# First tiles of both batch elements first, other-tile bias tables behind, and the softmax scaling on VectorE

## The chip, the cores and the metric

One core of one Trainium2 chip runs the whole program in one launch. The metric is device time in microseconds (us), the median of three runs of the same program. Engines: PE (TensorE matmul), PEld (its weight loads), DVE (VectorE), ACT (ScalarE), POOL (GpSimd) and SP (SyncE, which here only starts transfers).

## The reference

Attention with global and local keys and distance biases, then a dense gated feed-forward, then a feed-forward of one expert per token.

```
scores = q @ k.T / sqrt(64) - slope[h] * dist      # dist = n_local for global keys out of the window
keep   = (key < n_global) | (0 <= row - key < n_local)       # 8 and 96
x      = softmax(scores where keep) @ v                      # 2 batch elements, 8 heads, 768 rows
y      = (silu(x @ w_gate) * (x @ w_val)) @ w_out            # 1536 tokens, 512 -> 1536 -> 512
e      = argmax(y @ r_gate)
out    = p[e] * sigmoid(y @ r_out)[e] * relu(y @ w1[e]) @ w2[e]
```

## The kernel before, in words

**Tiles.** The rows of each batch element are six tiles of 128: tiles 0 to 5 and 6 to 11. With 96 local and 8 global keys a tile needs its own keys and those of one other tile: the tile before it, whose first 32 columns are overwritten by the first 32 keys of the batch element. The first tile of a batch element (0 and 6) needs its own keys only. Its scores are 128 wide, those of all others 256.

**Steps.** The loop at L781 makes 48 steps of attention, four for each of twelve positions (a pair of heads `j` of position `i`). Before the change position i is tile i. A step s issues, in this order: the scaling by the row sums of step s-1 (`att_R`), the tables `scale_tab`, the scores of step s (`att_S`), the products with v of step s-4 (`att_V`), the transposes of the exponentials of step s-3 (`att_P`), and in two of four steps the transposes of the next position's k and q (`att_T`). `att_X` turns a finished position into the input of the first feed-forward, and `load_qk` and `load_v` fetch later ones.

**Scores.** `att_S` (L283) multiplies in three parts, because k and q are split into a high and a low part (`khi`, `klo`, `qh`, `ql`) for accuracy. Each head of a pair has one bank (`ps_s0`, `ps_s1`) with no second buffer, so the scores of a step wait until VectorE's pass over the step before (L287: adds the bias table, takes the row minimum `mn`) has read the bank. ScalarE takes the exponential (L291) with its row sums `sm`; `att_R` has VectorE make 1/sum (`rs`, L227 and L320) and GpSimd multiply both heads by it:

```
nc.gpsimd.tensor_tensor(out=sp[:, :, 0:nw], in0=sp[:, :, 0:nw], in1=rs.to_broadcast([P, 2, nw]), op=ALU.mult)
```

**Bias tables.** `tab` holds own, other and own distances side by side (L233 to L241), `tab0` those of a first tile. `scale_tab(j, 0)` has ScalarE scale `tab0` for two heads; `scale_tab(j, 1)` has VectorE scale `tab`, 384 wide, in steps `TL` to `TL + 3`, with `TL = 2`.

**Beside it.** Weights come as 1 MB pieces of 64-bit numbers that are made 32-bit in four passes: L352 on ScalarE, L353, L358 and L361 on VectorE; L369 and L370 then split them. Up to step 13 (`GO`) PE gets start-up matmuls (`spin`, L147) between these; from step 13 on each step also issues two or three pieces of the first feed-forward (`m1_up` L387, `m1_down` L418 to L420), whose part `lo` is made on GpSimd (L399) in its first third. From step 13 every second step has SP write zeros to a buffer (`clear_rows`, L461). SP's transfers are issued in order: loads of q, k and v, `clear_rows`, and the reload of the first 32 rows of v (L332) for each position that is not a first tile. GpSimd issues the weight loads (L121) and copies the first 32 keys (L276, L277).

**Order.** The engines' instruction lists come from a scheduler that takes the program's order as a priority and moves instructions forward that are ready early. Within an engine the list is fixed.

The change touches `bt`, `load_v`, `att_T`, `window`, `att_S`, `att_R`, `att_V`, the table code and the loop:

Of the kernel before, what the change touches and what calls it, by code (L numbers as in the profile page):

```python
# [31 lines left out]
def attn_moe_moe_kernel(  # L32
# [224 lines left out]
    sp_t = {}  # L257

    def window(i):
        b, t = bt(i)  # L260
# [4 lines left out]
        own_first = s < o
        lo, hi = min(s, o), max(s, o)
        sl = slice(lo, hi + 1, hi - lo)
        return sl, ([0, 1] if own_first else [1, 0]), (tabs[:, :, 0:2 * P] if own_first else tabs[:, :, P:3 * P])

    def att_S(i, j):  # L270
# [997 lines left out]
```

## Time and profile before

| what | us |
|---|---|
| median of three runs | 684.61 |
| lowest and highest run | 683.14, 685.48 |
| span of the profiled execution, first to last instruction | 682.6 |
| PE busy | 656.2 |
| DVE busy | 406.9 |
| ACT busy | 299.3 |
| POOL busy | 134.4 |

The page gives for the profiled execution its span alone and no time of its own beside it. In the rows "x" is a count. [...] "idle before" is the time that the engine stood still, with what ended it.

### The profile page before, as it was taken

Reading aid. Unit: us, or ns where it says so; the run is one execution under the profiler, and the core shown is the slowest. Engines: PE = TensorE matmul, PEld = TensorE weight load, DVE = VectorE, ACT = ScalarE, POOL = GpSimd, SP = SyncE. Lnnn points to the kernel's source line nnn. Section 1 sums busy time; section 2 is a strip of 40 time slices with the busy share of each in tenths; the row PEclk is TensorE's granted clock in tenths of the full one; section 3 lists DMA queues with packets and bytes.
Section 4 is the critical chain, followed back from the end, with each engine's and each line's share of the span. In section 5 each row is a group of like instructions: output and inputs, shape, how many; then the busy total and the mean of one; then the engine's idle time right before and its main releaser. Section 6 shows DMA issues by size and latency. Waiting matters only on the chain. (4 is left out here: it accounts for less than half of the span.)

```text
span 682.6 us, 12065 instructions
## 1 busy us (share of the span) xinstructions
PE 656.2 (96%) x4645; PEld 571.4 (84%) x4645; DVE 406.9 (60%) x1007; ACT 299.3 (44%) x675; POOL 134.4 (20%) x180
## 2 busy tenths in 40 slices
PE   8999899999999999999999999998989999999993
PEld 7777687777788889999999999996878988998892
DVE  6689797564548887333464545466587656665120
ACT  5487575555535553111342222234466545555110
POOL 3245363433322320000000111011410110011011
PEclk8599999999999999999999999999999999999997
DMA  9666574220005464000040111122798666652000
GB/s 219 155 164 182 178 219 131 65 51 21 21 5 185 127 218 151 1 1 1 16 170 1 63 63 63 48 90 76 245 315 309 214 205 229 223 207 80 0 26 28
DMA packets 70674, 81.30 MB, mean 119 GB/s; under 512 B 43469, under 2 KB 43469, under 8 KB 70608
## 3 DMA queue, kind: packets, MB, share of 16 engines
q1 hardware_dynamic: 62304, 51.06, 24.8%
q0 software_dynamic: 8304, 29.39, 12.5%
q8 instruction: 38, 0.62, 0.4%
q14 instruction: 28, 0.23, 0.1%
HBM read 66.77 MB, written 14.72 MB: 119 GB/s over the span
## 5 line engine op out<-in xcount | busy, mean ns | idle before, releaser
L387 PE MATMUL ps_gv<-xhi,whi 128*128 128x256 f32 x576 | 168.1, 292 | 0.0
L387 PE MATMUL ps_gv<-xlo,whi 128*128 128x256 f32 x576 | 164.4, 285 | 0.0
L387 PE MATMUL ps_gv<-xhi,wlo 128*128 128x256 f32 x576 | 164.1, 285 | 0.0
L387 PEld LDWEIGHTS ps_gv<-xhi,whi 128*128 128x128 f32 x576 | 110.1, 191 | 6.3 <-issue 0.7
L387 PEld LDWEIGHTS ps_gv<-xlo,whi 128*128 128x128 f32 x576 | 110.3, 191 | 3.9 <-issue 1.0
L387 PEld LDWEIGHTS ps_gv<-xhi,wlo 128*128 128x128 f32 x576 | 110.5, 192 | 0.4
L575 DVE TENSOR_TENSOR wlo<-raw,whi 128x512 fp32r<-128x512 f32 (+1 forms) x104 | 81.9, 809 | 33.5 <-ACT whi L572 33.0
L572 ACT CAST whi<-raw 128x512 fp32r<-128x512 f32 (+1 forms) x104 | 72.0, 718 | 54.6 <-PE ps_gv L882 23.7
L394 DVE SCALAR_TENSOR_TENSOR hh<-th,ps_gv 128x256 f32<-128x256 f32 x72 | 30.0, 417 | 83.4 <-ACT th L392 83.4
L392 ACT ACTIVATE th<-ps_gv 128x256 f32<-128x256 f32 x72 | 27.4, 381 | 95.0 <-PE ps_gv L387 94.8
L321 POOL TENSOR_TENSOR sp<-sp,rs 128x512 f32<-128x512 f32 (+1 forms) x48 | 50.4, 1051 | 72.7 <-DVE rs L320 48.6
L882 PE MATMUL ps_gv<-sh,whi 128*128 128x256 f32 x224 | 62.9, 281 | 0.0
L882 PE MATMUL ps_gv<-sh,wlo 128*128 128x256 f32 x224 | 62.8, 281 | 0.0
L882 PE MATMUL ps_gv<-sl,whi 128*128 128x256 f32 x224 | 62.8, 280 | 0.0
L291 ACT ACTIVATE sp<-sp,mn 128x256 f32<-128x256 f32 (+1 forms) x96 | 46.6, 487 | 26.0 <-DVE mn L287 22.3
L398 ACT CAST hi<-hh 128x256 fp32r<-128x256 f32 x72 | 29.1, 405 | 60.7 <-DVE hh L395 56.8
L546 POOL DMA_INDIRECT xs<-ypay,rw x12 | 12.9, 1073 | 211.0 <-DVE rw L230 192.8
L287 DVE CUSTOM_DVE_ANT_0 sp<-ps_s,tabs 128x256 f32<-128x256 f32 (+1 forms) x96 | 35.9, 393 | 16.9 <-PE ps_s L283 16.0
L882 PEld LDWEIGHTS ps_gv<-sh,whi 128*128 128x128 f32 x224 | 42.3, 189 | 0.4
L882 PEld LDWEIGHTS ps_gv<-sl,whi 128*128 128x128 f32 x224 | 42.3, 189 | 0.4
L882 PEld LDWEIGHTS ps_gv<-sh,wlo 128*128 128x128 f32 x224 | 42.4, 189 | 0.0
L418 PE MATMUL ps_y<-whi,hi 128*128 128x512 f32 x96 | 40.1, 417 | 1.1 <-ACT hi L398 1.1
(241 smaller groups left out, 1355.3 us busy)
## 6 DMA issues: line engine op xcount, KB each, us to landing
raw<-in_moe_w_dram SPq DMA_DIRECT2D x30, 1024.0 KB, 5.2
raw<-in_moe_w_out_dram POOLq DMA_DIRECT2D x6, 1024.0 KB, 5.6
raw<-in_moe_w_gate_dram POOLq DMA_DIRECT2D x5, 1024.0 KB, 5.8
raw<-in_moe_w_val_dram POOLq DMA_DIRECT2D x5, 1024.0 KB, 5.8
xs<-ypay SPq DMA_DIRECT2D x8, 514.0 KB, 5.8
xr<-xs POOLq DMA_DIRECT2D x7, 514.0 KB, 5.8
ytok<-ypay SPq DMA_DIRECT2D x12, 257.0 KB, 3.3
ypay<-in_k_dram SPq DMA_DIRECT2D x12, 256.0 KB, 3.7
```

Of the source, the lines that this page charges most:

```text
L287: nc.vector.tensor_tensor_reduce(out=sp[:, e, 0:nw], in0=pS[e][:, 0:nw], in1=tb[:, h0 + e, :], scale=-QS, scalar=3.0e38, op0=ALU.add, op1= ...
L291: nc.scalar.activation(out=sp[:, e, 0:nw], in_=sp[:, e, 0:nw], func=AF.Exp, bias=mn[:, i, h0 + e:h0 + e + 1], scale=-1.0, accum_out=sm[:, ...
L321: nc.gpsimd.tensor_tensor(out=sp[:, :, 0:nw], in0=sp[:, :, 0:nw], in1=rs.to_broadcast([P, 2, nw]), op=ALU.mult)
L387: nc.tensor.matmul(o, a[:, kk, fo:fo + P], x[c][:, kk, :], start=(kk == 0 and m == 0), stop=(kk == KD - 1 and m == 2))
L392: nc.scalar.activation(out=th, in_=pg[:, 0, :], func=AF.Tanh, scale=0.5)
L394: nc.vector.scalar_tensor_tensor(out=hh, in0=th, scalar=1.0, in1=pg[:, 0, :], op0=ALU.add, op1=ALU.mult)
L398: nc.scalar.copy(hi, hh)
L418: nc.tensor.matmul(o, hi[:, sl], wh, start=first, stop=False)
L546: put = [nc.gpsimd.indirect_dma_start(out=xs, out_offset=bass.IndirectOffsetOnAxis(ap=rw[:, z].bitcast(U32), axis=0), in_=pay[:, z], in_of ...
L572: ins = nc.scalar.copy(hv[:, o], raw[:, o])
L575: nc.vector.tensor_tensor(out=lv[:, o], in0=raw[:, o], in1=f(hv[:, o]), op=ALU.subtract)
L882: nc.tensor.matmul(ph[:, fo, :], a[:, kk, fo * P:(fo + 1) * P], x[:, kk, :], start=(kk == 0 and m == 0), stop=(kk == KD - 1 and m == 2))
```

## The change

The positions are tiles 0, 6, 1 to 5 and 7 to 11 in this order. Position 1 is tile 6, a first tile, with 128-wide scores; its keys stay in the buffer `xhi[5]`, its v in `ypay[:, 8]`, until tile 7 (position 7) has used them. Since they don't lie beside tile 7's own keys, `att_S` makes two runs of 128 columns there in place of one of 256. The copies of first keys and the reload of v are left out for the second tile of a batch element, whose other tile holds these already (`t > 1`). `kgh` and `kgl` hold the first keys of both batch elements. `TL` is 4, and the three instructions that make the middle of `tab` are called in step 4. `att_R` multiplies on VectorE, one head at a time. `tokid` and the row numbers of `ytok` follow the new order.

```diff
-TL = 2
+TL = 4
...
+    SEQ = [b * NT for b in range(B)] + [b * NT + t for b in range(B) for t in range(1, NT)]
     def bt(i):
-        return i // NT, i % NT
+        return SEQ[i] // NT, SEQ[i] % NT
+    def prev(i):
+        return SEQ.index(SEQ[i] - 1)
+    def slot(i):
+        return max(0, i - 1) % 3
+    def k_of(i):
+        if i == 1:
+            return xhi[NCH - 1][:, :, 0:P], xhi[NCH - 1][:, :, P:2 * P]
+        return khi[:, slot(i)], klo[:, slot(i)]
...
+    def other_tab():
+        ts(ta, before_, NL, BIG, ALU.is_ge, ALU.mult)
+        tt(tab[:, P:2 * P], ta, before_, ALU.add)
+        ts(tab[:, P:P + GW], tg[:, 0:GW], NL, None, ALU.add)
...
+    def runs_of(i):
+        at = window(i)[0]
+        if len(at) == 1 or 1 in at:
+            return [(n * P, P, *(lambda r, j, k=k: k[r, j, :] for k in k_of(x))) for n, x in enumerate(at)]
+        a, z = (slot(x) for x in at)
+        return [(0, 2 * P, *(lambda r, j, k=k: k[r, a:z + 1:z - a, j, :] for k in (khi, klo)))]
...
-        if j == 0 and t > 0:
-            o = (i - 1) % 3
-            nc.gpsimd.tensor_copy(khi[:, o, :, 0:GW], f(kgh))
-            nc.gpsimd.tensor_copy(klo[:, o, :, 0:GW], f(kgl))
+        if j == 0 and t > 1:
+            o = slot(prev(i))
+            nc.gpsimd.tensor_copy(khi[:, o, :, 0:GW], f(kgh[:, b]))
+            nc.gpsimd.tensor_copy(klo[:, o, :, 0:GW], f(kgl[:, b]))
...
-        for m, (a, x) in enumerate(((qh, khi), (qh, klo), (ql, khi))):
-            for e in range(2):
-                r = slice(64 * e, 64 * e + 64)
-                nc.tensor.matmul(pS[e][:, 0:nw], a[r, j, :], x[r, sl, j, :], start=(m == 0), stop=(m == 2))
+        for o, n, kh, kl in runs_of(i):
+            for m, (a, x) in enumerate(((qh, kh), (qh, kl), (ql, kh))):
+                for e in range(2):
+                    r = slice(64 * e, 64 * e + 64)
+                    nc.tensor.matmul(pS[e][:, o:o + n], a[r, j, :], x(r, j), start=(m == 0), stop=(m == 2))
...
-        nc.gpsimd.tensor_tensor(out=sp[:, :, 0:nw], in0=sp[:, :, 0:nw], in1=rs.to_broadcast([P, 2, nw]), op=ALU.mult)
+        for e in range(2):
+            ts(sp[:, e, 0:nw], sp[:, e, 0:nw], rs[:, e, :], None, ALU.mult)
...
-            if t > 0:
-                nc.sync.dma_start(out=v_t[i - 1][0:GW], in_=v[b, :, 0:GW, :].rearrange("h p d -> p h d"))
+            if t > 1:
+                nc.sync.dma_start(out=v_t[prev(i)][0:GW], in_=v[b, :, 0:GW, :].rearrange("h p d -> p h d"))
...
         if TL <= s < NPAIR + TL:
+            if s == TL:
+                other_tab()
             scale_tab(s - TL, 1)
```

How the order moves, first on VectorE at its table of distances, ahead of the first scores. The last three instructions of the tables before `klo`, in the changed kernel (`ypay` is the scratch that holds `tab`, L247 and L250 are the helpers `ts` and `tt`):

```order
L256 SCALAR_TENSOR_TENSOR ypay<-ypay,ng 128x128
L247 TENSOR_SCALAR ypay<-ypay,ng 128x128
L250 TENSOR_TENSOR ypay<-ypay 128x128
L247 TENSOR_SCALAR ypay<-ypay,ng 128x32
L220 TENSOR_TENSOR klo<-ps_y,khi 128x512
L220 TENSOR_TENSOR ql<-ps_y,qh 128x512
L247 TENSOR_SCALAR tabs<-ypay 128x384 x2
```

The three instructions of `other_tab` stand where they stood before, ahead of `klo`, and the first two table scalings directly behind `ql`.

VectorE from step 1's score pass on (`rs` is 1/sum, `sp` the exponentials, `tabs` the scaled tables, ISA rows with `mn` are the score pass), before:

```order
L287 ISA sp,mn<-ps_s_306,tabs 128x128
L287 ISA mn 128x1
L320 RECIPROCAL rs<-rs 128x2
L287 ISA sp,mn<-ps_s_307,tabs 128x128
L287 ISA mn 128x1
L227 TENSOR_SCALAR tabs<-ypay 128x384 x3
L227 TENSOR_SCALAR rs<-sm 128x2
L227 TENSOR_SCALAR tabs<-ypay 128x384
```

and in the changed kernel:

```order
L316 ISA sp,mn<-ps_s_305,tabs 128x128
L316 ISA mn 128x1
L349 RECIPROCAL rs<-rs 128x2
L316 ISA sp,mn<-ps_s_306,tabs 128x128
L316 ISA mn 128x1
L247 TENSOR_SCALAR sp<-sp,rs 128x128 x2
L247 TENSOR_SCALAR tabs<-ypay 128x384 x2
L247 TENSOR_SCALAR rs<-sm 128x2
L247 TENSOR_SCALAR tabs<-ypay 128x384
```

Two multiplies come in behind each score pass, and one of the eight table scalings goes from here to step 4.

PE at the products with v of position 3, with what each row waits for (`vr` are the tiles of v: 761 and 754 the position's own, 572 and 580 the other one, whose first rows are reloaded; DMAHW is a transfer of SP), before:

```order
L387 MATMUL ps_gv_1099<-xhi0_81,wlo_912 128x256
L387 MATMUL ps_gv_1099<-xhi0_81,whi_911 128x256
L337 MATMUL ps_av_1041<-pT_990,vr_572 64x128 [waits DMAHW6_49]
L337 MATMUL ps_av_1041<-pT_990,vr_572 64x128
L337 MATMUL ps_av_1041<-pT_1052,vr_761 64x128 x2
```

and in the changed kernel:

```order
L417 MATMUL ps_gv_1097<-xhi0_81,wlo_907 128x256
L417 MATMUL ps_gv_1097<-xhi0_81,whi_906 128x256
L367 MATMUL ps_av_1038<-pT_986,vr_580 64x128 [waits DMAHW4_49,DVE_49]
L367 MATMUL ps_av_1038<-pT_986,vr_580 64x128
L367 MATMUL ps_av_1038<-pT_986,vr_754 64x128 [waits DMAHW3_49]
L367 MATMUL ps_av_1038<-pT_986,vr_754 64x128
```

The half with the reloaded rows is now the first of the position; before, the own half had been done some 20 rows ahead of it. On SP the reload stands behind a `clear_rows` in both.

## Rows read from the trace of the kernel before

**Rows 1.** The page: span, and part 1, busy us by engine (share, instructions).
```profile
span 682.6 us, 12065 instructions
...
PE 656.2 (96%) x4645; PEld 571.4 (84%) x4645; DVE 406.9 (60%) x1007; ACT 299.3 (44%) x675; POOL 134.4 (20%) x180
```

**Rows 2.** Stretches: length, PE, PEld, DVE, ACT, POOL busy (instructions), PEclk, DMA share, GB/s.
```profile
13.00:32.00 19.00, 19.00 (x111) 14.06 (x109) 13.01 (x39) 10.19 (x30) 5.08 (x8) 0.50 0.80 222
32.00:33.00 1.00, 1.00 (x5) 0.80 (x5) 0.78 (x5) 0.33 (x2) 0.05 (x1) 0.60 0.00 0
...
28.00:75.00 47.00, 43.16 (x333) 33.22 (x332) 42.13 (x106) 32.00 (x79) 22.95 (x25) 0.94 0.61 164
```

**Rows 3.** PE in order of time, 0 to 62 us: start, length, engine, line.
```profile
13.68 0.47 PE L283 MATMUL ps_s<-khi,qh 64*128 64x128 f32 x2
...
14.51 1.25 PE L147 MATMUL ps_gv<-ones 128*128 128x128 bf16 x10
...
28.44 0.58 PE L283 MATMUL ps_s<-khi,qh 64*128 64x256 f32 x1
...
29.38 0.71 PE L147 MATMUL ps_gv<-ones 128*128 128x128 bf16 x5
```

**Rows 4.** VectorE's groups, shapes apart, 28 to 75 us (last row 0 to 60).
```profile
L287 DVE CUSTOM_DVE_ANT_0 sp<-ps_s,tabs 128x256 f32<-128x256 f32 x25 | 10.1, 408 | 1.4 <-PE ps_s L283 1.4
L358 DVE SCALAR_TENSOR_TENSOR raw<-raw 128x1024 int32<-128x1024 int32 x5 | 9.1, 1814 | 0.0
L361 DVE SCALAR_TENSOR_TENSOR raw<-raw 128x1024 int32<-128x1024 int32 x4 | 6.7, 1666 | 0.0
L353 DVE TENSOR_SCALAR raw<-raw 128x1024 int32<-128x1024 int32 x5 | 5.4, 1082 | 0.0
...
L227 DVE TENSOR_SCALAR rs<-sm 128x2 f32<-128x2 f32 x12 | 3.5, 289 | 1.9 <-ACT sp L291 1.9
...
L287 DVE CUSTOM_DVE_ANT_0 sp<-ps_s,tabs 128x128 f32<-128x128 f32 x8 | 2.1, 282 | 0.3 <-PE ps_s L283 0.3
```

**Rows 5.** The same lines over the whole run: ns minimum/median/maximum.
```profile
L358 DVE SCALAR_TENSOR_TENSOR raw<-raw x18: 1200/1227/2057, 17.2 to 260.5; 128x1024 int32<-128x1024 int32 x18
...
L361 DVE SCALAR_TENSOR_TENSOR raw<-raw x18: 1205/1218/2040, 18.6 to 263.8; 128x1024 int32<-128x1024 int32 x18
...
L353 DVE TENSOR_SCALAR raw<-raw x18: 673/687/1434, 15.7 to 259.7; 128x1024 int32<-128x1024 int32 x18
...
L227 DVE TENSOR_SCALAR rs<-sm x48: 148/161/1006, 12.5 to 191.6; 128x2 f32<-128x2 f32 x48
```

**Rows 6.** GpSimd's groups, 28 to 75 us.
```profile
L321 POOL TENSOR_TENSOR sp<-sp,rs 128x512 f32<-128x512 f32 x13 | 15.3, 1177 | 15.8 <-DVE rs L320 13.6 <-PE ps_tr L194 1.6 <-DMA qr<-in_q_dram 0.6
```

**Rows 7.** PE in order of time: scores 128 wide, then 256 wide.
```profile
101.70 0.33 PE L283 MATMUL ps_s<-khi,qh 64*128 64x128 f32 x2
...
102.18 0.50 PE L419 MATMUL ps_y<-wlo,hi 128*128 128x512 f32 x1
...
125.00 0.38 PE L283 MATMUL ps_s<-khi,qh 64*128 64x256 f32 x2
...
125.55 0.39 PE L387 MATMUL ps_gv<-xhi,whi 128*128 128x256 f32 x1
```

**Rows 8.** VectorE in order of time: two table scalings and what follows.
```profile
11.35 0.62 DVE L227 TENSOR_SCALAR tabs<-ypay 128x384 bf16<-128x384 f32 x2
11.89 0.68 DVE L200 TENSOR_TENSOR klo<-ps_tr,khi 128x512 fp32r<-128x512 f32 x1
```

**Rows 9.** Waits of PE, 60 to 250 us: total, times, longest.
```profile
PE ps_y L420 <- POOL lo L399: 1.5, 4, 0.8
```

**Rows 10.** SP's queue, and PE, in order of time, at the longest wait.
```profile
62.64 1.91 SPq L461 DMA_DIRECT2D xs<-ypay  x1
64.65 0.56 SPq L332 DMA_DIRECT2D vr<-in_v_dram  x1
...
73.32 1.17 PE L337 MATMUL ps_av<-pT,vr 128*64 128x128 f32 x12 [2.87 <-DMA vr<-in_v_dram]
```

More of the change, by code (lines that the diff above doesn't have):

```diff
@@ L91, in attn_moe_moe_kernel @@
     xk = [ypay[:, NTILE - 3 + z, 0:DM].rearrange("p (h d) -> p h d", h=H) for z in range(2)]
+    SEQ = [b * NT for b in range(B)] + [b * NT + t for b in range(B) for t in range(1, NT)]
     def bt(i):
-        return i // NT, i % NT
+        return SEQ[i] // NT, SEQ[i] % NT
+    def prev(i):
+        return SEQ.index(SEQ[i] - 1)
+    assert B == 2
+    def slot(i):
[4 more added lines that the diff above has]
+        return khi[:, slot(i)], klo[:, slot(i)]
     q_t, k_t, v_t = {}, {}, {}
@@ L108, in load_v @@
         b, t = bt(i)
-        a = at_p.tile([P, H, HD], F32, tag="vr", name="vr", bufs=3)
+        if i == 1:
+            a = ypay[:, NTILE - 4, 0:DM].rearrange("p (h d) -> p h d", h=H)
+        else:
+            a = at_p.tile([P, H, HD], F32, tag="vr", name="vr", bufs=3)
         nc.sync.dma_start(out=a, in_=v[b, :, t * P:(t + 1) * P, :].rearrange("h p d -> p h d"))
@@ L178, in attn_moe_moe_kernel @@
     klo = at_p.tile([P, 3, NPAIR, P], F32R, name="klo", bufs=1)
-    kgh = at_p.tile([P, NPAIR, GW], F32R, name="kgh", bufs=1)
-    kgl = at_p.tile([P, NPAIR, GW], F32R, name="kgl", bufs=1)
+    kgh = at_p.tile([P, B, NPAIR, GW], F32R, name="kgh", bufs=1)
+    kgl = at_p.tile([P, B, NPAIR, GW], F32R, name="kgl", bufs=1)
     qT = {}
@@ L184, in att_T @@
         b, t = bt(i)
-        s = i % 3
+        kh, kl = k_of(i)
         qs = q_t.pop(i)
@@ L189, in att_T @@
         kr = k_t.pop(i)
-        for src, hi, lo in ((kr, khi[:, s], klo[:, s]), (qs, qh, ql)):
+        for src, hi, lo in ((kr, kh, kl), (qs, qh, ql)):
             yield
@@ L202, in att_T @@
         if t == 0:
-            nc.gpsimd.tensor_copy(kgh, f(khi[:, s, :, 0:GW]))
-            nc.gpsimd.tensor_copy(kgl, f(klo[:, s, :, 0:GW]))
+            nc.gpsimd.tensor_copy(kgh[:, b], f(kh[:, :, 0:GW]))
+            nc.gpsimd.tensor_copy(kgl[:, b], f(kl[:, :, 0:GW]))
     list(att_T(0))
@@ L237, in attn_moe_moe_kernel @@
     nc.scalar.copy(tab[:, 2 * P:3 * P], tab[:, 0:P])
-    ts(ta, before_, NL, BIG, ALU.is_ge, ALU.mult)
-    tt(tab[:, P:2 * P], ta, before_, ALU.add)
-    ts(tab[:, P:P + GW], tg[:, 0:GW], NL, None, ALU.add)
+    def other_tab():
+        ts(ta, before_, NL, BIG, ALU.is_ge, ALU.mult)
+        tt(tab[:, P:2 * P], ta, before_, ALU.add)
+        ts(tab[:, P:P + GW], tg[:, 0:GW], NL, None, ALU.add)
     def scale_tab(j, t):
@@ L260, in window @@
         b, t = bt(i)
-        s = i % 3
         if t == 0:
-            return slice(s, s + 1), [0], tabs[:, :, 3 * P:4 * P]
-        o = (i - 1) % 3
[L265 to L268, printed above, removed]
+            return [i], [0], tabs[:, :, 3 * P:4 * P]
+        if prev(i) == 1 or slot(i) < slot(prev(i)):
+            return [i, prev(i)], [0, 1], tabs[:, :, 0:2 * P]
+        return [prev(i), i], [1, 0], tabs[:, :, P:3 * P]
+    def runs_of(i):
[4 more added lines that the diff above has]
+        return [(0, 2 * P, *(lambda r, j, k=k: k[r, a:z + 1:z - a, j, :] for k in (khi, klo)))]
     def att_S(i, j):
@@ L330, in att_V @@
             av_t[i] = ps_tile("av", [P, NPAIR, P])
-            if t > 0:
-                nc.sync.dma_start(out=v_t[i - 1][0:GW], in_=v[b, :, 0:GW, :].rearrange("h p d -> p h d"))
+            if t > 1:
+                nc.sync.dma_start(out=v_t[prev(i)][0:GW], in_=v[b, :, 0:GW, :].rearrange("h p d -> p h d"))
         av = av_t[i]
         for w, src in enumerate(order):
-            vt = v_t[i] if src == 0 else v_t[i - 1]
+            vt = v_t[i] if src == 0 else v_t[prev(i)]
             for e in range(2):
@@ L456, in attn_moe_moe_kernel @@
     tokid = cst.tile([P, NTILE], I32, name="tokid")
-    nc.gpsimd.iota(tokid, pattern=[[P, NTILE]], base=0, channel_multiplier=1)
+    nc.gpsimd.iota(tokid[:, 0:B], pattern=[[S, B]], base=0, channel_multiplier=1)
+    for b in range(B):
+        o = B + b * (NT - 1)
+        nc.gpsimd.iota(tokid[:, o:o + NT - 1], pattern=[[P, NT - 1]], base=b * S + P, channel_multiplier=1)
     nc.gpsimd.tensor_copy(ids[:, 0:NTILE - 1], tokid[:, 0:NTILE - 1])
@@ L764, in m1_stream @@
                     for z in range(2):
-                        nc.sync.dma_start(out=ytok[(i + z) * P:(i + z + 1) * P, :], in_=ypay[:, i + z, :])
+                        nc.sync.dma_start(out=ytok[SEQ[i + z] * P:(SEQ[i + z] + 1) * P, :], in_=ypay[:, i + z, :])
                     if c == NCH - 2:
```

1 line of the change is left out of this document (removed).

## Prediction

> **What bounds the kernel now.** I read the page first, then the stretches of the granted clock, then PE's instructions in time, then VectorE's groups. The page gives 682.6 us of span, with PE busy for 656.2 of it [rows 1]: from end to end TensorE is the engine that sets the time, and what the change touches lies in the first 135 us or so. A step below is one `att_S`, a pair of heads of one position; there are 48, and position i has steps 4i to 4i+3.
>
> Two things cost PE time early on. [...] Second VectorE: between 28 and 75 us it is busy for 42.13 of 47 us [rows 2], with the score pass, the splitting of weights and all else in one queue, so PE often starts its next scores there when VectorE frees a bank.
>
> VectorE is itself slowed in that stretch. The weight passes L358, L361 and L353 average 1.81, 1.67 and 1.08 us and the two-element L227 0.289 us [rows 4]; their medians over the whole run, most of it with an idle GpSimd, are 1.23, 1.22, 0.69 and 0.161 [rows 5]. The company is GpSimd: its 13 multiplies L321 take 1.18 us each in the stretch [rows 6].
>
> **What the new order does not give.** It only permutes PE's work. By step 33 both programs have issued the same scores (but for one case below), transposes, start-up matmuls and feed-forward matmuls. So a first feed-forward that starts earlier is no gain in itself: four narrow steps early (4 to 7) are repaid by four wide ones at steps 24 to 27. The time changes only by (1) PE work that is added, (2) PE time at the low clock, (3) PE time with nothing to do. Each part of the change is priced as one of these.
>
> **The change part by part.**
>
> *Scores of tile 7 (PE work added).* Its other tile is tile 6, whose keys now lie apart, so a step issues 12 matmuls of 128 columns instead of 6 of 256. Six of 128 take 0.48 us (101.70 to 102.18), six of 256 take 0.55 (125.00 to 125.55) [rows 7]. Twice 0.48 less 0.55 is 0.41; the second six follow matmuls of their own kind, for which I take off 0.1. 0.3 by four steps is **+1.2 us** (ends: 0.3, if only the columns count and they are the same, and 1.6).
>
> *Low clock.* [...]
>
> *Scaling on VectorE.* Two `tensor_scalar` a step, one for each head (128x256, or 128x128 in a narrow step), replace one L321. No row has a VectorE multiply of 256 elements by a column. The nearest is the table scaling, 384 elements: two of them from 11.35 to 11.89, when the next instruction starts [rows 8], so 0.27 us each; I take 0.2 for 256, 0.4 a step. The other end is 0.41 each, the score pass of 128x256, which reads two inputs [rows 4]. For the 13 multiplies of the stretch that adds 5.2 us. Taken away is the company of L321: 5 x 0.59 + 4 x 0.45 + 5 x 0.39 + 12 x 0.13 = 8.3 us of slowing [rows 4, 5]. Of GpSimd's 22.95 busy us there L321 has 15.3 [rows 2, 6]; the rest, part of it only DMA issues, stays, so I count 80%, 6.6 us. Net -1.4. The narrow steps shorten the score pass too: 8 x (0.41 - 0.28) = 1.0 us [rows 4], all of it before 75 us. VectorE has 2.4 us less to do where it is full, and PE gets perhaps 60% of that: **-1.5 us** (ends: -2.4, and +3.1 with 0.41 each, which adds 10.7 for the 6.6 and the 1.0).
> [...]
>
> *GpSimd relieved.* PE waited 1.5 us in four places for `lo` (L399) [rows 9], which queues behind those multiplies of 1.18 us. Without them: **-1.3 us** (ends -1.5 and 0). The weight loads issued from GpSimd and its key copies lose the same neighbours, but they wait for `wlo` of VectorE and for PE, so 0.
>
> *Bias tables later.* By the order of instructions this hardly happens: `other_tab` still stands ahead of the first `klo`, and seven of the eight wide scalings stay ahead of the score pass of step 2; one moves to step 4. 0.
>
> *Loads and copies.* The loads of q, k and v are as many and as large, in the same places of SP's queue. The reload of the first v rows and the two first-key copies go for tiles 1 and 7; PE's waits do not name the copies, and the one long wait on a reload is another's. 0.
>
> *That wait.* PE stood 2.87 us, until 73.32, for 64 KB of v, issued at 64.65 behind a 514 KB `clear_rows` (62.64) on SP's queue [rows 10]. In the new order the reload of position 3 stands behind the same `clear_rows`, and the matmul that needs it comes first among its position's, no longer after the own half. So it stays: 0 (ends -2.9 and +1.5).
>
> Sum: 1.2 - 1.0 - 1.5 - 1.3 = -2.6 us. The profiled execution has a span of 682.6; the median of the three runs is 684.6, 2.0 above, which I leave as it is: **682.0 us**.
>
> **Rivals.**
> *Nothing but a permutation.* The low clock ends at the same moment, and PE, which keeps its order, finds other waits in place of VectorE's. Only +1.2 and -1.3 are left: 684.5. For it: PE is shown busy for 43.16 of the 47 us anyway [rows 2]. Chance 0.23.
> *Both stalls shrink.* [...] Chance 0.17.
> *VectorE becomes the bound (slower).* A multiply costs 0.41, and two stand between two score passes, the second of which frees a bank for PE. Then +3.1 replaces -1.5 and the clock gives nothing: 684.6 + 1.2 - 1.3 + 3.1 = 687.6. It decides from about 0.35 us a multiply. For it: VectorE is 90% busy there already [rows 2]. Against it: the table scaling [rows 8]. Chance 0.11.
> *The clock stays low for longer (slower).* Narrow steps leave PE less between two answers of VectorE, and these come later by the multiplies. PE held 0.50 for 19 us though its rows show no break [rows 2], so a few more microseconds are possible. Each costs half: 7 us more are +3.5, and the -1.0 goes: 686.5. [...] Chance 0.07.
>
> **How the numbers follow.** My forecast has 0.42; its own range is 680.5 to 683.5. No change means within 0.3%, 2.05 us, about what a measurement of this kernel can tell. Of the forecast 0.30 lies below 682.55 and 0.12 above. Faster: 0.30 + 0.17 = 0.47. Same: 0.12 + 0.23 = 0.35. Slower: 0.11 + 0.07 = 0.18. The range goes from 677.0, below both stalls shrunk, to 686.5, and leaves out most of the slower rivals.
>
> **What would show it.** Right: L358, L361 and L353 near their medians between 28 and 75 us, multiplies at 0.2 to 0.3 us, no waits for `lo`, the clock risen by about 30 us, the first feed-forward some 4 us earlier, but step 33 only 2 to 3 us earlier. Wrong: a multiply over 0.35 us from start to start, a granted clock of 0.50 well beyond 33 us, or a wait for v of another size.

## The result and the profile after

The changed kernel is **slower**. Four executions have a median of 691.68 us (690.91 to 694.87), beside 683.88 (682.15 to 685.48) for four of the kernel before: a ratio of 1.0146, 95% interval 1.0104 to 1.0187. Ten more executions in a later set gave 689.16 us and 1.0095 (1.0056 to 1.0133). The prediction was 682.0 us, with a range of 677.0 to 686.5. Single executions of one and the same kernel lie up to 13 us apart here (125 executions of the kernel before: 674.9 to 688.1, median 682.7), so ratios with their intervals decide below, not single times. The intervals leave out executions that lie over 1.5% above the fastest of their kernel, which in e8 (three of twelve) and e12 (eight of twelve) makes the ratio too low: over all executions the means there give 1.0094 and 1.0072.

The page of the changed kernel (its profiled execution took 692.3 us), span, part 1 and the granted clock of TensorE in 40 slices (PEclk, in tenths of its full speed):
```profile
span 690.6 us, 12005 instructions
...
PE 663.2 (96%) x4669; PEld 577.3 (84%) x4669; DVE 424.3 (61%) x1103; ACT 297.9 (43%) x675; POOL 83.4 (12%) x130
...
PEclk8588999899999999999999999999999999999997
```
Against [rows 1] VectorE has 17 us more and GpSimd 51 less, as the change says, and PE is busy for 7.0 us more of a span 8.0 us longer. PE's additional work is four split steps, so the rest of its additional busy time must be slowness. The stretches show it. Before, from start to start of each change of the clock (columns: length, then busy us of PE, PEld, DVE, ACT, POOL, then PEclk, DMA share, GB/s):
```profile
12.30:32.80 20.50, 20.30 (x117) 15.14 (x114) 14.49 (x48) 10.76 (x32) 5.53 (x10) 0.50 0.77 219
32.80:73.75 40.95, 37.11 (x302) 28.56 (x302) 37.25 (x94) 30.58 (x74) 20.89 (x23) 1.00 0.64 173
73.75:77.20 3.45, 3.45 (x23) 3.12 (x18) 2.34 (x4) 1.04 (x4) 1.03 (x1) 0.51 0.80 249
77.20:210.00 132.80, 131.53 (x1051) 104.27 (x1051) 84.05 (x271) 72.97 (x201) 52.53 (x65) 1.00 0.31 85
...
473.10:476.55 3.45, 3.06 (x28) 2.93 (x28) 3.05 (x22) 1.87 (x7) 0.00 (x0) 0.51 0.02 5
```
The changed kernel, the same view; its last row answers to the third of [rows 2]:
```profile
12.70:36.70 24.00, 24.00 (x138) 18.08 (x137) 17.65 (x70) 13.11 (x38) 1.11 (x2) 0.50 0.74 199
36.70:50.25 13.55, 12.14 (x112) 9.15 (x112) 11.86 (x44) 11.68 (x32) 2.24 (x3) 1.00 0.61 176
50.25:57.20 6.95, 6.90 (x30) 5.68 (x31) 5.83 (x17) 1.94 (x6) 0.75 (x1) 0.51 0.44 150
57.20:122.00 64.80, 62.80 (x482) 49.33 (x481) 55.53 (x168) 41.69 (x107) 11.34 (x16) 1.00 0.61 171
122.00:128.90 6.90, 6.65 (x37) 5.06 (x36) 4.87 (x13) 1.58 (x5) 0.58 (x1) 0.51 0.18 41
...
28.00:75.00 47.00, 45.18 (x335) 35.61 (x334) 37.50 (x119) 29.49 (x78) 6.63 (x9) 0.84 0.56 156
```
The first low stretch is 3.5 us longer, the short one at 74 us is gone, and there are two new ones of 6.9 us. With half of the time at 0.50 counted as lost, an estimate from the granted clock, they make (24.0 + 6.95 + 6.9 - 20.5 - 3.45) / 2 = 7.0 us. In a row of 128x256 matmuls of the changed kernel (L417), one follows the other in 0.21 us at 0.50 (125.32 to 126.17 us, records of 0.41 us that overlap) and in 0.12 at 1.00 (299.74 to 301.54, records of 0.28): a loss of 43% there, by which it would be 6.0 us. The last product of attention with v is issued at 209.5 us instead of 202.9, 6.6 later. The stretch of the kernel before at 473 us has no counterpart in the changed kernel and takes 1.7 us back, so of the 8.0 us between these two spans 5.2 by the half lie in low stretches and the rest elsewhere. In [rows 2] VectorE has 42.13 us of 47; here 37.50, and PE stands 1.8 us in that stretch against 3.8. So what the prediction wanted of VectorE came about, and in these two executions more than that is lost at the low clock.

Ahead of each new stretch PE stands. PE in order of time (the bracket: idle before it, and what ended that):
```profile
46.36 0.66 PE L335 MATMUL ps_y<-ident,sp 128*128 128x128 f32 x4
48.08 0.35 PE L312 MATMUL ps_s<-khi,qh 64*128 64x256 f32 x1 [1.06 <-DVE rs L349]
...
50.30 0.58 PE L312 MATMUL ps_s<-khi,qh 64*128 64x256 f32 x1
...
117.75 0.33 PE L312 MATMUL ps_s<-khi,qh 64*128 64x128 f32 x2
...
118.89 0.66 PE L335 MATMUL ps_tr<-ident,sp 128*128 128x128 f32 x4 [0.25 <-ACT pT L338]
...
120.24 0.33 PE L312 MATMUL ps_s<-khi,qh 64*128 64x128 f32 x1 [0.57 <-DVE mn L316]
...
121.11 0.32 PE L312 MATMUL ps_s<-khi,qh 64*128 64x128 f32 x1 [0.21 <-DVE mn L316]
```
What VectorE did while PE waited for it at 47 us, in order of time:
```profile
45.68 0.62 DVE L247 TENSOR_SCALAR sp<-sp,rs 128x256 f32<-128x256 f32 x2
46.20 1.22 DVE L391 SCALAR_TENSOR_TENSOR raw<-raw 128x1024 int32<-128x1024 int32 x1
47.34 0.26 DVE L247 TENSOR_SCALAR rs<-sm 128x2 f32<-128x2 f32 x1
47.51 0.41 DVE L316 CUSTOM_DVE_ANT_0 sp<-ps_s,tabs 128x256 f32<-128x256 f32 x1
```
Two multiplies (0.52 us from start to start) and a pass over weights stood ahead of the score pass at 47.51, which frees the bank that PE wants for its next scores. PE's bracket names the reciprocal L349, which follows that pass on VectorE.

### The profile page after: what moved, and what is told of

The parts are those of the page before. It is cut to its first block, busy times and chain, and to the rows that moved or that the text cites. A ratio compares the mean times of both kernels' runs of the same rounds, so it can differ in the third digit from the quotient of the medians.

```text
span 690.6 us, 12005 instructions
## 1 busy us (share of the span) xinstructions
PE 663.2 (96%) x4669; PEld 577.3 (84%) x4669; DVE 424.3 (61%) x1103; ACT 297.9 (43%) x675; POOL 83.4 (12%) x130
## 5 line engine op out<-in xcount | busy, mean ns | idle before, releaser
L417 PE MATMUL ps_gv<-xhi,whi 128*128 128x256 f32 x576 | 168.4, 292 | 0.3 <-ACT xhi L373 0.3
L417 PE MATMUL ps_gv<-xhi,wlo 128*128 128x256 f32 x576 | 165.5, 287 | 0.3 <-DVE wlo L400 0.3
L417 PE MATMUL ps_gv<-xlo,whi 128*128 128x256 f32 x576 | 165.0, 286 | 0.0
L417 PEld LDWEIGHTS ps_gv<-xhi,whi 128*128 128x128 f32 x576 | 110.6, 192 | 6.8 <-issue 1.0
L417 PEld LDWEIGHTS ps_gv<-xlo,whi 128*128 128x128 f32 x576 | 110.8, 192 | 3.7 <-issue 0.4
L417 PEld LDWEIGHTS ps_gv<-xhi,wlo 128*128 128x128 f32 x576 | 111.0, 193 | 2.1 <-issue 0.6
L316 DVE CUSTOM_DVE_ANT_0 sp<-ps_s,tabs 128x256 f32<-128x256 f32 (+1 forms) x96 | 36.7, 394 | 7.9 <-PE ps_s L312 6.1
L450 PE MATMUL ps_y<-whi,lo 128*128 128x512 f32 x96 | 37.9, 405 | 1.2 <-POOL lo L429 1.1
L579 POOL DMA_INDIRECT xs<-ypay,rw x12 | 13.5, 1126 | 209.5 <-DVE rw L250 190.7
```

The source lines that it names most:

```text
L316: nc.vector.tensor_tensor_reduce(out=sp[:, e, 0:nw], in0=pS[e][:, 0:nw], in1=tb[:, h0 + e, :], scale=-QS, scalar=3.0e38, op0=ALU.add, op1= ...
L417: nc.tensor.matmul(o, a[:, kk, fo:fo + P], x[c][:, kk, :], start=(kk == 0 and m == 0), stop=(kk == KD - 1 and m == 2))
L450: nc.tensor.matmul(o, lo[:, sl], wh, start=False, stop=last)
```

## The experiments

Span times mean granted clock is an estimate of what an execution would take at the full clock, as if all of it went with TensorE; the rest of the span is the time lost at the low one (the low clock where the kernel runs out is part of it: in the seven profiles followed to their end it begins between 672.0 and 686.0 us, at 674.5 in the kernel before and 681.8 in the changed one). Both are worked out for each execution, and the means with standard errors over all executions are below. Ratios are against the kernel before in the same set. The sets ran on five chips, between which the kernel before differs by up to 1.6 us at the full clock and 1.3 lost, so differences of that size from its pooled row say little.

| kernel | median us | ratio, 95% interval | full clock | lost |
|---|---|---|---|---|
| before (125 executions) | 682.7 | | 666.0 ± 0.2 | 14.8 ± 0.3 |
| changed (14 executions) | 690.3 | two sets, above | 666.9 ± 0.5 | 21.6 ± 1.4 |
| e1 order alone | 686.25 | 1.0058 (1.0031 to 1.0085) | 666.1 ± 0.5 | 18.4 ± 0.3 |
| e2 multiplies alone | 689.61 | 1.0115 (1.0065 to 1.0165) | 668.4 ± 0.8 | 18.9 ± 1.1 |
| e3 tables early | 689.98 | 1.0136 (1.0082 to 1.0190) | 667.6 ± 0.3 | 20.8 ± 1.4 |
| e4 split alone | 685.49 | 1.0046 (1.0011 to 1.0082) | 667.4 ± 0.9 | 16.3 ± 1.1 |
| e5 copies to ScalarE | 685.22 | 1.0016 (0.9985 to 1.0047) | 667.2 ± 0.7 | 15.8 ± 1.3 |
| e6 VectorE loaded | 688.12 | 1.0078 (1.0050 to 1.0106) | 668.4 ± 0.3 | 18.1 ± 0.5 |
| e7 half the multiplies | 685.89 | 1.0026 (0.9994 to 1.0057) | 666.9 ± 0.6 | 16.2 ± 1.1 |
| e8 more start-up matmuls | 689.24 | 1.0057 (1.0020 to 1.0094) | 677.4 ± 0.7 | 10.5 ± 0.8 |
| e10 bridged stands | 684.58 | 1.0018 (0.9990 to 1.0046) | 670.5 ± 0.5 | 11.9 ± 0.7 |
| e11 filled narrow steps | 691.20 | 1.0114 (1.0079 to 1.0148) | 672.7 ± 1.0 | 17.0 ± 1.7 |
| e12 e5 and e7 together | 688.37 | 0.9986 (0.9937 to 1.0035) | 667.4 ± 0.6 | 18.1 ± 1.8 |
| e13 multiplies early | 691.24 | 1.0121 (1.0077 to 1.0165) | 669.8 ± 0.9 | 19.3 ± 1.9 |
| e14 multiplies late | 693.69 | 1.0155 (1.0116 to 1.0193) | 669.4 ± 0.7 | 21.8 ± 1.2 |
| e15 copies, old order | 685.61 | 1.0052 (1.0023 to 1.0081) | 667.9 ± 0.4 | 16.4 ± 0.9 |
| e16 old order, tile 1 narrow | 680.88 | 0.9969 (0.9942 to 0.9997) | 661.9 ± 0.6 | 16.4 ± 1.1 |
| e17 clearings moved | 688.36 | 1.0070 (1.0030 to 1.0109) | 668.4 ± 0.5 | 16.9 ± 1.1 |
| e18 reload by ScalarE | 692.59 | 1.0133 (1.0085 to 1.0182) | 669.9 ± 0.7 | 20.2 ± 1.1 |

The first two rows of the table are the finding: 7.6 us between the medians, and 6.8 more lost at the low clock in the mean.

**The two halves of the change: e1, e2.** e1 undoes the multiplies in the changed kernel, e2 does them alone in the kernel before.
```diff
-        for e in range(2):
-            ts(sp[:, e, 0:nw], sp[:, e, 0:nw], rs[:, e, :], None, ALU.mult)
+        nc.gpsimd.tensor_tensor(out=sp[:, :, 0:nw], in0=sp[:, :, 0:nw], in1=rs.to_broadcast([P, 2, nw]), op=ALU.mult)
```


> The changed kernel with one thing undone: the multiply by the reciprocal goes back to GpSimd. In the trace of the changed kernel TensorE's granted clock is 0.50 from 50.3 to 57.1 us and from 122.0 to 128.8 us, each time behind waits of about 1 us for VectorE; the kernel before has neither stretch. Theory A (the multiplies on VectorE make its score passes late, TensorE stands, and its clock falls): both stretches go, 3.4 us each, and the 1.6 us of waits at 118 to 122, so about 691.5 - 8 = 683.5, near the kernel before; the first low stretch (12.8 to 36.7) stays. Theory B (the order of the tiles does it): both stretches stay, 690 to 692.

> The kernel before with the multiply on VectorE alone, old order of tiles. Theory A (the multiplies make VectorE late): low stretches of the clock appear behind waits for VectorE between 40 and 130 us, and the time is 687 to 692. Theory B (the order does it): no new low stretch, multiplies of about 0.27 us from start to start, L358 and L361 at 1.2 us, 681 to 684.

e1's stretches:
```profile
12.70:40.00 27.30, 27.30 (x150) 20.60 (x150) 18.52 (x65) 15.48 (x46) 9.19 (x12) 0.50 0.74 200
40.00:135.00 95.00, 92.49 (x760) 73.32 (x761) 77.80 (x214) 62.04 (x162) 43.42 (x49) 1.00 0.56 158
```
As theory A has it, both new stretches are gone, but the time is 3 us above the kernel before: the first stretch is longer still, 27.3 us. In e2 it is short (17.1 us), and another stretch stands behind a wait of 3.3 us, for v:
```profile
12.90:30.00 17.10, 17.10 (x108) 13.42 (x107) 12.30 (x50) 8.92 (x24) 1.91 (x3) 0.50 0.78 205
30.00:108.50 78.50, 70.61 (x575) 55.36 (x573) 67.62 (x215) 53.58 (x138) 13.38 (x21) 1.00 0.69 187
108.50:115.30 6.80, 5.44 (x29) 4.37 (x28) 3.33 (x9) 3.00 (x7) 0.00 (x0) 0.50 0.28 65
```
e2's multiplies did relieve its weight passes (L359 and L362 1.22 us each, 28 to 75 us, and in e1, with GpSimd multiplying, the same lines 1.48 and 1.55), and yet PE stands longer. So each half costs, 0.6% and 1.2%, and neither theory holds alone. Of e1's cost all that shows is lost at the low clock (18.4 against 14.8), of e2's about two thirds.

**The smaller parts: e3, e4.** e3 makes the tables ahead of the loop; e4 splits tile 7's scores in the kernel before.
```diff
-TL = 4
+TL = 2
...
+    other_tab()
+
     def scale_tab(j, t):
...
-            if s == TL:
-                other_tab()
```


> The changed kernel with the bias tables for the other tile's keys made ahead of the loop and scaled from step 2 again. Both theories, and the prediction's zero for this part: within 1 us of the changed kernel (690.5 to 692.5), with the same three low stretches of the clock. If the tables matter for the first low stretch (12.8 to 36.7), its end moves by several us and the time by half as much.

```diff
+        if i == 7:
+            cut = [(n * P, slice(k, k + 1)) for n, k in enumerate(sorted((i % 3, (i - 1) % 3)))]
+        else:
+            cut = [(0, sl)]
+        for o, z in cut:
+            n = P if i == 7 else nw
...
-                nc.tensor.matmul(pS[e][:, 0:nw], a[r, j, :], x[r, sl, j, :], start=(m == 0), stop=(m == 2))
+                    nc.tensor.matmul(pS[e][:, o:o + n], a[r, j, :], x[r, z, j, :], start=(m == 0), stop=(m == 2))
```


> The kernel before with the scores of tile 7 alone issued as 12 matmuls of 128 columns in place of 6 of 256, as the changed kernel does. By the prediction's term +1.2 us (0.3 to 1.6): 685. If the split itself brings on the low clock at 122 us, a stretch of 0.50 appears near steps 28 to 31 and the time is 688 or more.

e3 lies within what the changed kernel scatters: the tables cost nothing that shows, as predicted, though with six executions a cost of 2 us would not show. Its profile, the fastest of the six, does not have the three low stretches that I expected: the first is 17.8 to 34.9 us, one lies at 116.8 to 123.7, and behind PE's stand of 1.05 us at 46 us there is none. e4 is 1.4 us up at the full clock and shows no stretch at steps 28 to 31; its interval, 0.8 to 5.6 us, holds the predicted 1.2.

**VectorE relieved, halved, loaded: e5, e7, e6, e12, e15.** e5 and e15 (in the changed kernel, and in the one before):
```diff
-        if j % 2 == 0 or i < 4:
+        if j % 2 == 0 or i < 8:
             nc.scalar.copy(pT[:, :, 0:n, :], pt[:, :, 0:n, :])
```


> The changed kernel with the copies of the transposed exponentials that VectorE does (0.69 us each, every second step of positions 4 to 7) given to ScalarE, so that VectorE loses what the multiplies added there. By the runs so far the time splits into span times mean granted clock (666 us for the kernel before and for the changed one alike) and the rest, lost to the low clock (14.5 and 24.3 us). Theory A (late score passes of VectorE make TensorE stand, and its clock falls behind that): the low stretch near 120 us becomes rarer, the lost part falls by 2 to 4 us and the time is 687.5 to 690. Theory C (the lost time has nothing to do with VectorE's load in that stage): unchanged, 691 to 692.5.

> The kernel before with the copies of the transposed exponentials of positions 4 to 7 on ScalarE, multiplies on GpSimd as before. Theory A says that VectorE makes no low stretch in this kernel (its two long stands are for DMA), so nothing is to be won: 682 to 685, lost 14 to 16. If VectorE's load matters there too: 679 to 681.

e7, and e12 with e5's edit as well:
```diff
-        for e in range(2):
-            ts(sp[:, e, 0:nw], sp[:, e, 0:nw], rs[:, e, :], None, ALU.mult)
+        ts(sp[:, 0, 0:nw], sp[:, 0, 0:nw], rs[:, 0, :], None, ALU.mult)
+        nc.gpsimd.tensor_tensor(out=sp[:, 1, 0:nw], in0=sp[:, 1, 0:nw], in1=rs[:, 1, :].to_broadcast([P, nw]), op=ALU.mult)
```


> The changed kernel with the multiply of one head of each pair on GpSimd and of the other on VectorE. Theory A: half the addition to VectorE's queue, between the changed kernel (691.7) and the one with all multiplies on GpSimd (686.3): 688 to 690. If the two halves hide beside each other better than either alone, 685 or less.

> The changed kernel with both reliefs of VectorE: one head's multiply on GpSimd, and the copies of the transposed exponentials of positions 4 to 7 on ScalarE. Theory A: VectorE has less in its queue than in the kernel before, the lost part falls to 13 to 15 us: 681 to 685. If the reliefs overlap, as one of the two: 685 to 686.

e6, in the kernel before:
```diff
+    junk = cst.tile([P, 4], F32, name="junk")
...
+        if s in (12, 31):
+            for z in range(4):
+                nc.vector.tensor_reduce(out=junk[:, z:z + 1], in_=sp_t[((s - 2) // NPAIR, (s - 2) % NPAIR)], axis=AX.XY, op=ALU.max)
```


> The kernel before, order and multiplies as they were, with four extra reductions of 128x512 on VectorE (some 0.55 us each) ahead of the score passes of step 12 and of step 31; their results are used nowhere. Theory A: TensorE stands for 1 to 2 us at step 12 and the clock falls behind it, so the time grows by more than the stand itself: 1.5 us of standing and 3 to 5 us lost to the low clock, 687 to 689. Theory C (only the stand counts): 684 to 685, the lost part stays at 14.5 us.

Either relief of VectorE wins back some 4 to 5 us of the changed kernel's 7.6 (e5 685.2, e7 685.9, more than expected), nearly all of it in the lost part. Together they win no more: e12's mean is 687.3 us, with 18.1 ± 1.8 lost, which its errors don't tell from e5 and e7. In its profile, the slowest of twelve, it is ScalarE, with the copies, that is late, and the low clock follows. PE in e12:
```profile
109.11 0.66 PE L214 MATMUL ps_tr<-ident,qr 128*128 128x128 f32 x4 [2.55 <-ACT pT L338]
...
122.58 0.55 PE L214 MATMUL ps_tr<-ident,ypay 128*128 128x128 f32 x3 [0.90 <-ACT pT L338]
```
with 0.50 from 111.0 to 114.4 and from 124.7 to 128.1. e15 has the same wait, 3.15 us at 105.65, with 0.50 from 106.4 to 113.3; it wins nothing, and lies just above theory A's figures. e5 shows the limit of theory A: PE stands 0.97 us at 47 us as in the changed kernel, and no low stretch follows. e6 missed its aim: its reductions ran behind the score passes of step 12, and the stand there stayed at 0.37 us. The time grew by 5 us all the same, with a stand of 3.3 us for v near 105 us and 0.50 from 107.4 to 117.6. It doesn't tell A from C.

**The first low stretch: e8, e10, e11, e16.** e8 in the kernel before, with 10 for 4 in both calls of a step (one is shown); e10 is its second half alone:
```diff
-            spin(4)
+            spin(10)
...
+            if i == 0 and j == 0 and m < 2:
+                spin((12, 4)[m], pin=True)
```


> The kernel before with more start-up matmuls on ones: 10 in place of 4 in each of the two places of steps 0 to 12, and 16 more within the first score step, where TensorE stands for 0.8 and 0.3 us. Theory D (the first low stretch, 17 to 27 us long in all profiles, follows the thin work of the first steps): it gets shorter or vanishes, the lost part falls from 14.5 to about 6 us, while 156 matmuls of about 0.06 us add up to 9 us where TensorE has no gaps: 676 to 686. If the low stretch does not hang on that, the added work alone shows: 690 or more.

> The kernel before with only the 16 start-up matmuls more within the first score step, over the stands of 0.8 and 0.3 us there, and none later. Theory D1 (the stands at 9 to 10.5 us bring on the first low stretch): it starts later or is shorter, the lost part falls from 14.6 to 8 to 11 us, the added work is 0 to 0.5 us: 677 to 681. Theory D2 (the thin work of steps 1 to 8 does it, whatever the stands): the first low stretch stays some 20 us, 683 to 684.

e8's stretches, then e10's:
```profile
8.00:21.00 13.00, 9.32 (x120) 7.86 (x121) 10.84 (x36) 6.91 (x25) 2.94 (x6) 1.00 1.09 268
21.00:24.40 3.40, 3.40 (x30) 2.74 (x27) 2.74 (x12) 2.44 (x8) 1.68 (x3) 0.50 0.70 148
24.40:41.00 16.60, 15.71 (x195) 12.66 (x195) 12.81 (x38) 12.38 (x32) 8.21 (x10) 1.00 0.53 148
```
```profile
8.00:20.40 12.40, 9.27 (x106) 7.21 (x103) 10.79 (x40) 7.99 (x28) 3.19 (x7) 1.00 1.14 277
20.40:30.60 10.20, 10.15 (x55) 7.61 (x55) 6.11 (x19) 6.13 (x17) 3.58 (x4) 0.50 0.78 207
30.60:41.00 10.40, 10.38 (x96) 7.92 (x94) 9.54 (x30) 8.43 (x22) 4.50 (x6) 1.00 0.34 78
```
Over twelve executions each, the lost part falls to 11.9 in e10, where filler bridges two stands of 0.8 and 0.3 us, and to 10.5 in e8, from 14.8: the time at the low clock does change with what PE does in its first steps. The lengths of these two stretches show less, for with the usual filler single profiles have 3.4 us (e7), 6.8 us (e17) and a start at 17.7 us (e15) too. Neither pays: the filler adds 4.5 us in e10 (far more than expected) and 11.4 in e8, for 2.9 and 4.3 us of lost time.

e11 is e1 with the filler in steps 4 to 7, again in both calls; e16 makes steps 4 to 7 narrow in the old order, by leaving out tile 1's work with the other tile's keys:
```diff
-            spin(4)
+            spin(8 if 4 <= s < 8 else 4)
```


> The order of the changed kernel with all multiplies on GpSimd (686.3 us, lost 18.4) and 8 start-up matmuls more in each of steps 4 to 7, which are narrow in the new order. Theory N (the narrow steps' thin work makes the first low stretch longer, 27 us in that profile against 20.5 before): it gets shorter by about 7 us, the lost part falls by 2 to 4 us, the matmuls add 1.8 to 3.5 us: 685 to 687. If the lost part stays at 18.4, the narrow steps are not it: 688 to 690.

```diff
-        if t == 0:
+        if t == 0 or i == 1:
             return slice(s, s + 1), [0], tabs[:, :, 3 * P:4 * P]
```


> The kernel before with tile 1 computed from its own keys alone (the scores, transposes and products with the other tile's keys are left out), so that steps 4 to 7 are narrow as in the new order, in the old order otherwise. The work left out is some 3 to 5 us at the full clock (span times mean clock 662 to 664). Theory N (narrow work there makes the first low stretch longer): it ends no earlier than in the kernel before though there is less to do, 24 to 27 us instead of 20, and the lost part rises to 17 to 19: 680 to 683. Otherwise the lost part is 13 to 15.5 and the time 676 to 679.

In e11 the first stretch is 13.6 us (12.1 to 25.7) against e1's 27.3, as theory N says, but stands for v of 2.2 and 3.6 us come with 0.50 again. Over its six executions nothing is won: 17.0 ± 1.7 lost against e1's 18.4, and 6.6 us more at the full clock, where I expected 1.8 to 3.5. In e16 it is 23.9 us against 20.5, which e4 has too with steps 4 to 7 wide, and the lost part is 1.6 us up, less than expected and hardly beyond the errors: it speaks weakly for N and doesn't prove it.

**Which stage: e13, e14.** Multiplies on VectorE in positions 0 to 2 alone, then from position 3 on alone (`i >= 3`):
```diff
+        if i < 3:
             for e in range(2):
                 ts(sp[:, e, 0:nw], sp[:, e, 0:nw], rs[:, e, :], None, ALU.mult)
+        else:
+            nc.gpsimd.tensor_tensor(out=sp[:, :, 0:nw], in0=sp[:, :, 0:nw], in1=rs.to_broadcast([P, 2, nw]), op=ALU.mult)
```


> The changed kernel with the multiplies on VectorE in positions 0 to 2 (steps 0 to 11) only, later ones on GpSimd. Theory A with its place at steps 24 to 31: the low stretch at 120 us is absent, the lost part is near the 18.4 of all on GpSimd, 685 to 687.5. If the place is the first steps: lost 20 to 24, 688 to 692.

> The changed kernel with the multiplies on GpSimd in positions 0 to 2 and on VectorE from position 3 on. Theory A with its place at steps 24 to 31: stands for VectorE or ScalarE between 100 and 122 us with a low stretch behind them, lost 20 to 24, 688 to 692. If the place is the first steps: lost near 18.4, 685 to 687.5.

Both are as slow as the whole, so the loss belongs to no one place; my expectation of a single place fell. e13 has the stand of step 12 and its stretch again, though at 120 us there is none:
```profile
50.60:57.40 6.80, 6.80 (x29) 5.57 (x30) 6.02 (x14) 1.86 (x6) 1.79 (x2) 0.50 0.48 153
57.40:105.00 47.60, 45.16 (x344) 35.47 (x342) 41.00 (x104) 32.46 (x79) 21.34 (x25) 1.00 0.72 193
105.20:108.60 3.40, 3.38 (x21) 2.62 (x23) 0.92 (x6) 2.23 (x7) 1.28 (x2) 0.50 0.42 143
```
Its third row stands behind a wait for v of 2.0 us. e14 has no stand at step 12, but one of 2.6 us for v near 70 us with 0.50 from 71.6 to 78.4, and the stretch at 126.2 to 133.0.

**The wait for v in the kernel before: e17, e18.**
```diff
-        elif s < GO + 2 * NE and (s - GO) % 2 == 0:
-            clear_rows((s - GO) // 2)
+        elif s < GO + 2 * NE and (s - GO) % 4 < 2:
+            clear_rows((s - GO) // 4 * 2 + (s - GO) % 4)
```


> The kernel before with the eight clearings of rows (514 KB each on SyncE's queue) issued at the ends of steps 13, 14, 17, 18 and so on, in place of 13, 15, 17, 19, so that none stands right ahead of the reload of v. Theory A (a stand of TensorE costs itself and the low clock behind it): the stand of 2.9 us near 70 us goes, with it the low stretch of 3.4 us behind it: about 4 us less, 677 to 680, lost 12.5 to 14, full-clock part 663.5 to 665. If the stand only moves or other transfers hold the reload up: 682 to 684.

```diff
-                nc.sync.dma_start(out=v_t[i - 1][0:GW], in_=v[b, :, 0:GW, :].rearrange("h p d -> p h d"))
+                nc.scalar.dma_start(out=v_t[i - 1][0:GW], in_=v[b, :, 0:GW, :].rearrange("h p d -> p h d"))
```


> The kernel before with the reload of the first rows of v issued on ScalarE's queue in place of SyncE's, where nothing else stands. Theory A: as for the clearings moved, 677 to 680, if the reload then lands in 2 to 3 us. Against it: the issue stands in ScalarE's order, behind copies and exponentials, and may come later there: 682 to 685 with a stand for v of another size.

Both missed; the wait moved to later positions. In e18 PE stood 2.95 us for v until 92.31, with 0.50 from 91.5 to 98.3. PE in e17:
```profile
63.82 0.44 PE L337 MATMUL ps_av<-pT,vr 128*64 128x128 f32 x4 [1.07 <-DMA vr<-in_v_dram]
...
99.97 1.12 PE L337 MATMUL ps_av<-pT,vr 128*64 128x128 f32 x8 [3.56 <-DMA vr<-in_v_dram]
```
and 0.50 from 99.8 to 106.7 behind the second. Whether a kernel without that wait would gain more than the wait stays open: in e2 and e6 it is absent at position 3, but a wait for v of 3.3 us stands near 105 us in its place. No version that does all of the work beats the kernel before.

**The changed kernel again: e9.**


> The changed kernel as it is, beside the others of this set, since its time so far rests on four executions. Theory A (its loss over the kernel before is time at the low clock): span times mean granted clock 666 to 668 as in the kernel before, the rest 20 to 25 us against 14.6: 688 to 692. In its second profile the low stretches behind TensorE's waits may lie elsewhere between 40 and 130 us, but there are some.

As expected, with 689.16 us and 20.5 lost. Its second profile has the first stretch at 11.3 to 38.6 us and one at 120.5 to 127.4; the stand of step 12 is there (1.0 us) without a low stretch.

Over all 20 profiles, a count of stretches of 0.50 between 41 and 140 us finds 26. In the 5 us ahead of each PE stands for 0.8 to 3.6 us in all; of all other moments there at the full clock, 8% have that much behind them. The waits are for VectorE, ScalarE or the DMA of v, whatever kernel it is. The length of the stand tells more: of 17 stands of 1.39 us or more that begin there at the full clock, each had a low stretch begin within 5 us of its start, and of 23 of 0.75 to 1.24 us six had (not so in e5 and e9). This is no rule for the whole run: 1.52 us at 40.4 us in e2 and 1.67 at 248.7 in e10 were followed by none. It is company, not proof of a cause, since no run took a stand away and left all else as it was; the nearest to one are e8 and e10, where filler in the stands lowered the lost time.

## Why the prediction was wrong

**The step that failed is "Low clock".** The -1.0 us of the sum, for a clock that rises earlier, was the author's estimate, and no run shows it. The rise came 3.9 us later (36.7 instead of 32.8), and the lost time measured +6.8 us over 14 executions (21.6 - 14.8, error 1.4), all low stretches together. The order's share is in e1's profile a longer first stretch: 27.3 us, and no other up to 140 us. Over the profiles with the usual filler the first stretch lasts 22.0 us on average in the new order (nine profiles, 3.4 to 27.3) and 17.1 in the old (seven, 6.8 to 23.9), a difference of 4.9 us with an error of 3.3, so these alone would not show it. The larger mistake lies beside the term: the working counted a stand of PE at its own length. Already in [rows 10] the stand of 2.87 us at 73.32 was followed by 3.4 us at 0.50, by the half another 1.7 us; I had the stand's row and priced the stand alone.

**The rivals.** "The clock stays low for longer" named the right resource and direction, at a chance of 0.07. That its 7 us more are e1's 27.3 against 20.5 is luck, as single profiles scatter far more, and the rival knew nothing of stretches after 41 us. The lost time of e8 and e10 (10.5 and 11.9 us with more filler, 14.8 without) and the stands before 26 stretches agree with it. "VectorE becomes the bound" had the mechanism of the second half, a score pass behind multiplies, with a wrong condition: the multiply took 0.26 us from start to start, not 0.35, and VectorE is less busy than before between 28 and 75 us (37.50 against 42.13). What stands in PE's way there is a single late score pass, not its load. "Nothing but a permutation" is refuted by e1. "Both stalls shrink" was right on the wait for v (below) and wrong on the clock.

**Scaling on VectorE, -1.5.** The relief came in full: VectorE's groups from 28 to 75 us, which answer to [rows 4]:
```profile
L247 DVE TENSOR_SCALAR sp<-sp,rs 128x256 f32<-128x256 f32 x16 | 5.0, 350 | 0.0
...
L388 DVE SCALAR_TENSOR_TENSOR raw<-raw 128x1024 int32<-128x1024 int32 x4 | 4.9, 1222 | 0.7 <-ACT raw L382 0.7
L391 DVE SCALAR_TENSOR_TENSOR raw<-raw 128x1024 int32<-128x1024 int32 x4 | 4.9, 1220 | 0.0
L383 DVE TENSOR_SCALAR raw<-raw 128x1024 int32<-128x1024 int32 x4 | 2.8, 688 | 0.0
```
They are at the medians of [rows 5], all of the slowing gone where I counted 80%. The multiply was mis-sized: 0.26 us from start to start (0.52 for two, above; the 350 ns here are one record's duration, and neighbours overlap: those two end at 46.30, the next instruction starts at 46.20) against my 0.2. The sign failed: e2, which has this half alone, is 6.9 us slower, 4.1 of it lost at the low clock and 2.4 of it at the full clock, where the prediction had a gain. That PE's stands are what cost it is argued from the traces, not shown.

**GpSimd relieved, -1.3.** Of 1.5 us in [rows 9], 1.1 remain, so 0.4 came. PE's waits in the changed kernel, 60 to 250 us:
```profile
PE ps_y L450 <- POOL lo L429: 1.1, 3, 0.6
PE ps_s L312 <- DVE mn L316: 0.8, 2, 0.6
...
PE ps_av L367 <- DMA vr<-in_v_dram: 0.3, 1, 0.3
```
**That wait, 0.** The last row is a later product, at 123 us: the wait of 2.87 us at position 3 went, near the end of -2.9. The product came only 0.2 us later (at 70.66 us, where PE began to wait at 70.45 before), but the reload landed sooner, 6.2 us after its issue instead of 8.6. On SP's queue nothing changed; the 1 MB weight load that GpSimd issues did. First the kernel before, then the changed one:
```profile
63.27 0.74 POOL L121 DMA_DIRECT2D raw<-in_moe_w_out_dram  x1 [1.37 <-DVE wlo L370]
...
64.16 0.54 SPq L362 DMA_DIRECT2D vr<-in_v_dram  x1
...
65.12 0.70 POOL L141 DMA_DIRECT2D raw<-in_moe_w_out_dram  x1
```
Before, the load was issued 1.4 us ahead of the reload (64.65, [rows 10]), now 1.0 us behind it. The other profiles go the same way: where the reload is issued at least 0.4 us ahead of the load, it lands in 5.9 to 6.4 us (seven profiles), and where it comes 1.4 to 2.2 us behind it, in 7.7 to 8.6 (four; 3.0 us behind it, in e8, in 6.2 again). The step named the `clear_rows` and left the load out. e1, e13 and e14 have waits for v again (0.9, 2.0 and 2.6 us), so it hangs on the rest of the timing.

**Tile 7, +1.2.** Right. One of its steps in the changed kernel:
```profile
130.58 0.33 PE L312 MATMUL ps_s<-khi,qh 64*128 64x128 f32 x2
...
131.40 0.39 PE L417 MATMUL ps_gv<-xhi,whi 128*128 128x256 f32 x1
```
From start to start these 12 matmuls take 0.82 us against 0.55 in [rows 7], 0.27 a step, 1.1 in all. **Tables and copies, 0:** right for the tables (e3); no wait names the copies.

Not settled: why the same kernel's low stretches differ from one execution to the next, why PE's stands and the low clock go together, and how much of the order's 3 us is the narrow steps' (e16 leaves 1.6 of lost time, with an error of 1.1) and how much the split (e4).

## What to carry to other kernels

A short stand of TensorE early in a kernel can cost more than its own length (1.06 us here, with 6.95 us at 0.51 behind it): look at the granted clock behind each stand of before, and price a new wait with the low stretch that may follow. Relieving an engine on average may not help if the instruction that frees TensorE's bank now queues behind the moved work (VectorE was busy for 37.50 us in place of 42.13, and the score pass at 47.51 came late all the same), so follow single instructions in the queue, not busy shares. For a transfer that PE waits for, look at the large ones that all queues issue just ahead of it, not only at its own queue (the reload landed in 8.6 us behind a 1 MB load of another queue, in 6.2 ahead of it). And where executions differ, split span into span times clock and the rest: the two parts told in one table what no single trace did.

## What the hardware showed that was not expected

A stand of about 1 us (1.06 at 48.08 us) can be followed by 6.95 us at 0.51 of the clock, an estimated 3.4 us lost or three times its own length, and in another execution of the same kernel (e9, 1.05 at 49.15) by nothing; between 41 and 140 us that happened to 6 of 23 stands of 0.75 to 1.24 us, and to all 17 of 1.39 us or more, whether PE waited for VectorE, ScalarE or a DMA. PE then shows busy throughout (6.90 of 6.95 us); what tells is the granted clock, and that one and the same matmul is longer (0.58 us at 50.30 against 0.35 at 48.08). Beside GpSimd's multiplies VectorE's weight passes took 1.48 and 1.55 us (e1), without them 1.22 (the changed kernel), and taking the multiplies away did not make the kernel faster. A reload of 64 KB landed 5.9 to 6.4 us after its issue where a 1 MB load was issued behind it, and 7.7 to 8.6 us where that load had gone 1.4 to 2.2 us ahead of it.
